# A seven-product expert layer: each product in its own PSUM bank, or summed there in chains

## The chip, the cores and the metric

The kernel runs on one core of a Trainium2 chip. The metric is device time in microseconds (us) for one execution; lower is better. Engines are named as in the profile: PE is TensorE, DVE is VectorE, ACT is ScalarE, POOL is GpSimd, SP is the queue that issues the DMAs. PSUM is the memory that TensorE writes; it has eight banks.

## The reference

Block-sparse attention gives `x` (3072 tokens, 512 features); a mixture of eight experts follows, in which every token goes through every expert and a balanced weight `P` sums the results.

```python
def _moe_ref(x, w_gate, w1, w2):
    ...
    for e in range(E):                       # 8 experts
        h = np.maximum(x @ w1[e], 0.0)       # 512 -> 1024
        ye = h @ w2[e]                       # 1024 -> 512
        out += P[:, e:e + 1] * ye
    return out.astype(np.float32)
```

Results are needed to float32 accuracy.

## The kernel before, in words

Attention comes first (lines 318 to 705) and writes `x` in pieces to DRAM. The rest, which this case is about, is the expert part: 32 blocks `i`, one for each of 8 experts and 4 batches of 768 tokens. Stage one of a block is `x @ w1` with its Relu, stage two is `h @ w2`.

Each matrix product is done by a scheme of Strassen's kind (Winograd's form): the operands are cut into two by two quadrants, and seven products of sums of quadrants replace eight. The products are numbered 0 to 6. Each float32 operand is held as a high and a low float16 half, so one product is three matmuls for each chunk of 128 (high-high, high-low, low-high).

**Stage one** (`stage1`, line 936) goes by four quarters `qi` of 128 hidden units. A product is 6 matmuls of 128x384 (line 945) into a bank of the pool `ps_h` (4 banks). The products come in the order of `PORDER`: 0, 1, 5, 6, 3, 4, 2. Each is combined with what came before: ACT copies product 0 out (line 990, tile a1), and DVE adds the others by `comb` (line 955), seven instructions a quarter since product 4 is read twice. Relu runs on ACT. From the four quadrants of the hidden layer (a1, u3, r11, c21) POOL makes the sums that stage two needs (`add`, lines 1017 and 843), and `emit` makes the halves of each operand of stage two: the high half on ACT (line 965), the low half on POOL for products 2, 3 and 5 and on DVE for the others (line 975; line 969 for product 1, whose Relu is folded in).

**Stage two** (`stage2`, line 1043) goes by product and by three chunks `ci` of 128 tokens. A chunk is 12 matmuls of 128x256 (line 1058) into a bank of `ps_y` (4 banks). DVE then adds it, times the token's weight, to the accumulators in SBUF (line 1079). The table `USES` says where to: product 0 goes to four quadrants in two instructions 512 wide, 5 to three, 4 to two, the others to one. For the first expert ACT copies product 0 out instead (line 1076).

**Order.** While stage two of block `i` runs, stage one of block `i + 1` is issued between its products (lines 1123 to 1174): products 0 and 1, quarter 0, product 5, quarter 1, products 6 and 3, quarter 2, products 4 and 2, quarter 3. Work that is less urgent (low halves, POOL sums, the weights of the next expert) is put in lists (`Slots`, line 758); `tick` is called after each product with an estimate of its cost and issues what fits, and `need` issues at once what the next step must have. Tile's scheduler then orders each engine's instructions by a simulated time line; on the chip each engine takes them in that order.

**At each change of expert** 2 MB of weights are loaded for each stage (`load_w`, line 152). DVE finds their largest value (line 170) and POOL reduces it over partitions (line 177); the scale follows from that. POOL makes sums of quadrants (line 836), and the seven operands are split into halves on ACT (line 821) and DVE (line 825): `split_w1` while the last block of the old expert runs, `split_w2` after it. The second weight is loaded into the buffer of the first, once all of that has been split.

Of the kernel before, what the change touches and what calls it, by code (L numbers as in the profile page):

```python
# [10 lines left out]
F32 = mybir.dt.float32  # L11
# [18 lines left out]
PORDER = (0, 1, 5, 6, 3, 4, 2)  # L30
NHT = 30
NU = 8
LOP = (2, 3)
LOPE = (2, 3, 5)
NLE = 99
# [24 lines left out]
def tile_sparse_attention_moe(  # L60
# [151 lines left out]
    def first_steps():  # L212
# [39 lines left out]
        for n, p in enumerate(PORDER[:4]):  # L252
            at(NTILE - NC * (4 - n // 2 * 2), lambda p=p: load_x1(0, p))
        split(TS1, 6, temp)
        split(TS1, 3, d)
        split(TS2, 4, c)
# [481 lines left out]
    ps_y = mpool("ps_y", 4, space=PSUM)  # L738
# [111 lines left out]
    def split_w1(e):  # L850
        a, s3 = wr["a"], wr["s3"]

        def one(p, src):
            queue_split(w1p[p], src, ("w1", e, p))

        one(0, a[0, 0])
        queue_sum(a[0, 0], a[1, 0], a[0, 0], ("w1", e, 5))
        one(1, a[0, 1])
        queue_sum(a[0, 1], a[0, 1], a[0, 0], ("w1", e, 2))
        one(5, a[0, 0])  # L860
        one(6, s3)
        one(3, a[1, 1])
        one(4, a[1, 0])
        one(2, a[0, 1])
# [70 lines left out]

    def stage1(i, qi):
        fs = slice(qi * P, (qi + 1) * P)
        lop = LOPE if i < NLE else LOP

        def product(p):  # L940
            slots.need(("w1", i // B, p))
            ps = ps_h.tile([P, 512], F32, tag="ph", name=f"p{p}_{i}_{qi}")[:, :TH]
            for kc in range(KH):
                for m, (l, r) in enumerate(((0, 0), (0, 1), (1, 0))):
                    nc.tensor.matmul(  # L945
                        ps, lhsT=w1p[p][:, l, kc, fs], rhs=xp[p][:, r, kc],
                        start=(kc == 0 and m == 0), stop=(kc == KH - 1 and m == 2),
                    )
            return ps
# [9 lines left out]
        def emit(p, src, relu=False, delay=0):  # L959
# [4 lines left out]
            def high():  # L964
                nc.scalar.activation(h[:, 0], src, AF.Relu if relu else AF.Copy)  # L965

            def low():
                if relu:
                    nc.vector.scalar_tensor_tensor(
                        out=h[:, 1], in0=src, scalar=0.0, in1=h[:, 0],  # L970
                        op0=ALU.max, op1=ALU.subtract,
                    )
                else:
                    eng = nc.gpsimd if p in lop else nc.vector
                    eng.tensor_tensor(out=h[:, 1], in0=src, in1=h[:, 0], op=ALU.subtract)  # L975
# [5 lines left out]
            if p in lop:  # L981
# [7 lines left out]
        a1 = fresh("a1")  # L989
        nc.scalar.activation(a1, product(0), AF.Copy, scale=HDOWN)  # L990
        tick(0, 1)
        r11 = fresh("r11")
        comb(r11, product(1), a1)
        nc.scalar.activation(r11, r11, AF.Relu)
        emit(0, r11)
        tick(1, 2)
        comb(a1, product(5), a1)
        tick(1, 0)
        u3 = fresh("u3")
        comb(u3, product(6), a1)  # L1000
        tick(1, 0)
        slots.settle(i, qi - 1)
        c21 = fresh("c21")
        comb(c21, product(3), u3)
        emit(1, c21, relu=True)
        tick(1, 1)
        p5 = product(4)
        comb(u3, p5, u3)
        comb(a1, p5, a1)
        nc.scalar.activation(u3, u3, AF.Relu)  # L1010
        emit(3, u3)
        tick(2, 2)
        comb(a1, product(2), a1)
        nc.scalar.activation(a1, a1, AF.Relu)  # L1014

        def add():
            nc.gpsimd.tensor_tensor(out=s1, in0=a1, in1=u3, op=ALU.add)  # L1017
            sub(a1, a1, r11)
            slots.need((("h", i, 0), i, qi))
            sub(r11, s1, r11)  # L1020
            slots.need((("h", i, 1), i, qi))
            nc.scalar.activation(c21, c21, AF.Relu)
            sub(c21, c21, r11)

        s1 = fresh("s1")
        slots.add(add, (("sum", i), i, qi), 1, act=0.41, pool=3.9)
        emit(4, s1, delay=SD[0])
        emit(6, a1, delay=SD[1])
        emit(5, r11, delay=SD[2])
        emit(2, c21, delay=SD[3])  # L1030
        tick(1, 1)

    USES = {
        0: ((0, None), (1, None)),
        1: ((0, 0),),
        5: ((0, 1), (1, None)),
        6: ((1, None),),
        3: ((1, 0),),
        4: ((0, 1), (1, 1)),
        2: ((0, 1),),  # L1040
    }

    def stage2(i, p):
        e, b = divmod(i, B)
        if p not in (0, 1, 3):
            slots.need(("sum", i))
        slots.need(("h", i, p))
        slots.need(("w2", e, p))
        if b == 0 and e:
            slots.need(("pwe", e))  # L1050
        for ci in range(CH):
            t0 = b * NC + ci
            ts = (t0, t0 + CH)
            py = ps_y.tile([P, 512], F32, tag="py", name=f"py_{i}_{p}_{ci}")[:, :DH]
            tsl = slice(ci * P, (ci + 1) * P)
            for kc in range(KF // 2):
                for m, (l, r) in enumerate(((0, 0), (0, 1), (1, 0))):
                    nc.tensor.matmul(  # L1058
                        py, lhsT=hs[i, p, kc][:, l, tsl], rhs=w2p[p][:, r, kc],
                        start=(kc == 0 and m == 0), stop=(kc == KF // 2 - 1 and m == 2),  # L1060
                    )
            if p == 0 and e == 1:
                for t in ts:
                    nc.scalar.activation(
# [140 lines left out]
```

## Time and profile before

| what | value |
|---|---|
| runs shown | 2587.79, 2589.89, 2609.31 us; median 2589.89 us |
| profiled execution, its span | 2589.7 us |
| chain that ended last, by engine | PE 59%, DVE 15%, POOL 9%, issue 8%, DMA 6%, ACT 2% |
| mean granted TensorE clock | 0.944 |
| HBM | 140.54 MB read, 17.30 MB written, 61 GB/s over the span |

In a line of the groups stand line, engine, operation, what is written and read (names of the program, buffer numbers left out), the shapes and the count; then the busy time in us, the mean duration of one in ns, and the idle time of the engine just before, with what ended it. In a line of the waits stand who waited for whom, the us in total, how many times, and the longest. In a line of the order of time stand the start and duration in us, the engine, the line and the instruction, and in brackets the idle time before it and what ended that. "Issue" is time in which the engine waited for nothing that the profile shows.

### The profile page before, as it was taken

How to read it: one execution, taken by the hardware profiler on the slowest of the kernel's cores; microseconds unless marked ns; L12 is line 12 of the kernel's file. 1: busy time of each engine (PE TensorE's matmuls, PEld its weight loads, DVE VectorE, ACT ScalarE, POOL GpSimd, SP SyncE). 2: the span in 40 equal slices, each digit the busy share in tenths (PEclk: the TensorE clock that was granted, in tenths of full speed). 3: DMA queues.
4: the chain of work that ended last, by engine and by line, in shares of the span. 5: the costliest groups of instructions: out<-in, count | busy, mean ns of one | idle time of the engine just before them, and what ended most of it. 6: DMA issues, size and time to landing. Idle time of an engine off the chain costs nothing.

```text
span 2589.7 us, 46975 instructions
## 1 busy us (share of the span) xinstructions
PE 2361.4 (91%) x18270; PEld 1678.2 (65%) x18270; DVE 2009.5 (78%) x3747; ACT 1277.7 (49%) x2234; POOL 1559.8 (60%) x1387
## 2 busy tenths in 40 slices
PE   6999999897879979998998999899989998998999
PEld 3656666564656657765775677577657765776777
DVE  6768788675767788788778878877887788778876
ACT  4466767664445544444454444444444444444442
POOL 4557687763754476457556655755476557556653
PEclk9967879787989989999999999999999999999999
DMA  5679999996111221122121212211221122121211
GB/s 167 141 154 190 190 186 197 182 203 134 58 68 44 76 76 44 44 76 76 48 82 62 87 47 76 76 44 44 76 76 44 44 76 76 57 73 60 84 68 50
DMA packets 363924, 236.38 MB, mean 91 GB/s; under 512 B 303772, under 2 KB 316084, under 8 KB 363700
## 3 DMA queue, kind: packets, MB, share of 16 engines
q1 hardware_dynamic: 362128, 230.59, 34.9%
q10 hardware_dynamic: 1572, 2.78, 0.6%
q8 instruction: 143, 2.34, 0.4%
q14 instruction: 81, 0.66, 0.1%
HBM read 140.54 MB, written 17.30 MB: 61 GB/s over the span
## 4 chain that ended last, share of the span: by engine, by line
PE 59%; DVE 15%; POOL 9%; issue 8%; DMA 6%; ACT 2%; SPq 0%; DVEq 0%; POOLq 0%; ACTq 0%
PE py L1058 24%; PE p L945 22%; PE sc L513 4%; PE sc L510 4%; PE u L577 3%; DMA pt<-ph 3%; POOL r L836 3%; DMA r<-in_moe_w_dram 3%; DVE mx_w L170 2%; DVE h L975 2%; DVE acc L1079 2%; POOL h L975 2%; DVE w1p L825 1%; DVE u L955 1%; DVE a L955 1%
## 5 line engine op out<-in xcount | busy, mean ns | idle before, releaser
L1058 PE MATMUL py<-w2p,h 128*128 128x256 f16 x8064 | 974.6, 276 | 59.9 <-DVE acc L1079 21.3
L1058 PEld LDWEIGHTS <-h 128*128 128x128 f16 x8064 | 795.0, 99 | 221.6 <-issue 23.9
L1079 DVE SCALAR_TENSOR_TENSOR acc<-py,spare,acc 128x256 f32<-128x256 f32 (+1 forms) x840 | 457.8, 580 | 50.6 <-PE py L1058 49.4
L945 PE MATMUL p<-arena 128*128 128x384 f16 x2304 | 424.5, 334 | 70.9 <-DVE c L955 34.2
L975 POOL TENSOR_TENSOR h<-u,h 128x384 f16<-128x384 f32 x128 | 135.0, 1055 | 571.4 <-ACT h L965 474.2
L945 PEld LDWEIGHTS <-w1p 128*128 128x128 f16 x3072 | 302.5, 99 | 215.6 <-issue 41.5
L945 PE MATMUL p<-x,w1p 128*128 128x384 f16 x2304 | 407.4, 328 | 15.7 <-ACT a L990 13.3
L945 PEld LDWEIGHTS <-arena 128*128 128x128 f16 x2304 | 229.3, 100 | 213.1 <-issue 89.4
L965 ACT ACTIVATE h<-c 128x384 f16<-128x384 f32 x256 | 132.2, 522 | 351.8 <-DVE c L955 275.3
L536 POOL TENSOR_TENSOR ph<-pe,ph 128x768 f16<-128x768 f32 x144 | 259.8, 1818 | 69.1 <-ACT ph L532 51.9
L518 DVE CUSTOM_DVE_ANT_0 pe<-sc,mask 128x768 f32<-128x768 f32 x192 | 182.6, 954 | 112.3 <-PE sc L513 92.1
L955 DVE SCALAR_TENSOR_TENSOR a<-p,a 128x384 f32<-128x384 f32 x384 | 210.7, 549 | 20.2 <-PE p L945 15.0
L523 ACT ACTIVATE pe<-pe,nm 128x768 f32<-128x768 f32 x192 | 174.9, 928 | 98.6 <-DVE nm L522 86.2
L510 PE MATMUL sc<-k,q 128*128 128x512 f32 (+1 forms) x384 | 199.2, 519 | 18.8 <-DVE nm L518 17.2
L513 PE MATMUL sc<-k,q 64*128 64x512 f32 (+1 forms) x384 | 200.8, 524 | 0.0
L965 ACT ACTIVATE h<-r 128x384 f16<-128x384 f32 x256 | 132.2, 521 | 97.9 <-POOL r L843 94.3
L1017 POOL TENSOR_TENSOR s<-a,u 128x384 f32<-128x384 f32 x128 | 141.0, 1101 | 51.0 <-ACT a L1014 51.0
L577 PE MATMUL u<-vh,pt 128*128 128x66 f16 x2304 | 149.3, 211 | 17.8 <-DMA pt<-ph 16.9
L843 POOL TENSOR_TENSOR r<-s,r 128x384 f32<-128x384 f32 x128 | 149.0, 1164 | 23.6 <-issue 14.0
L945 PE MATMUL p<-arena,w1p 128*128 128x384 f16 x768 | 149.5, 330 | 14.9 <-DVE a L955 9.6
L577 PEld LDWEIGHTS <-pt 128*128 128x128 f16 x3456 | 140.1, 109 | 30.4 <-DMA pt<-ph 18.7
L843 POOL TENSOR_TENSOR c<-c,r 128x384 f32<-128x384 f32 x128 | 149.5, 1168 | 9.2
(155 smaller groups left out, 3439.7 us busy)
## 6 DMA issues: line engine op xcount, KB each, us to landing
arena<-xd SPq DMA_DIRECT2D x124, 384.0 KB, 3.8
x<-xd SPq DMA_DIRECT2D x93, 384.0 KB, 4.1
r<-in_moe_w_dram SPq DMA_DIRECT2D x16, 2048.0 KB, 8.8
arena<-in_q_dram SPq DMA_DIRECT2D x16, 384.0 KB, 3.5
arena<-in_k_dram SPq DMA_DIRECT2D x16, 384.0 KB, 4.1
arena<-in_v_dram SPq DMA_DIRECT2D x4, 1536.0 KB, 8.6
xd<-xs_t SPq DMA_DIRECT2D x16, 384.0 KB, 3.0
out_dram<-acc SPq DMA_DIRECT2D x24, 256.0 KB, 2.0
```

The source lines that it names most:

```text
L510: nc.tensor.matmul(sc[:, lo:hi], lhsT=q1[:, qc], rhs=k1[:, lo:hi], start=True, stop=False)
L513: nc.tensor.matmul(sc[:, lo:hi], lhsT=q2[:D, qc], rhs=k1[:D, lo:hi], start=False, stop=True)
L518: nc.vector.tensor_tensor_reduce(out=pe, in0=sc[:, :S], in1=masks[c], scale=1.0, scalar=-FMAX, op0=ALU.add, op1=ALU.max, accum_out=nm,)
L536: eng.tensor_tensor(out=lo, in0=pe, in1=hi, op=ALU.subtract)
L577: nc.tensor.matmul(uv[:, c], lhsT=a[:, ci * NC + kc, :], rhs=w[:, h, kc, :], start=(kc == 0 and m == 0), stop=(kc == NC - 1 and m == 2),)
L843: nc.gpsimd.tensor_tensor(out=out, in0=x, in1=y, op=ALU.subtract)
L945: nc.tensor.matmul(ps, lhsT=w1p[p][:, l, kc, fs], rhs=xp[p][:, r, kc], start=(kc == 0 and m == 0), stop=(kc == KH - 1 and m == 2),)
L955: nc.vector.scalar_tensor_tensor(out=t, in0=ps, scalar=HDOWN, in1=other, op0=ALU.mult, op1=ALU.add)
L965: nc.scalar.activation(h[:, 0], src, AF.Relu if relu else AF.Copy)
L975: eng.tensor_tensor(out=h[:, 1], in0=src, in1=h[:, 0], op=ALU.subtract)
L1058: nc.tensor.matmul(py, lhsT=hs[i, p, kc][:, l, tsl], rhs=w2p[p][:, r, kc], start=(kc == 0 and m == 0), stop=(kc == KF // 2 - 1 and m == 2),)
L1079: nc.vector.scalar_tensor_tensor(out=dst, in0=src, scalar=c, in1=dst, op0=ALU.mult, op1=ALU.add)
```

## The change

Stage one keeps three banks a quarter: x, y and z. Product 0 opens x; products 5, 6 and 3 are added onto it in PSUM (no `start` flag), and ACT reads the running sum after each (r11's share, a1, u3, c21). Product 1 alone is in y and is added to r11 by DVE. Product 4 opens z and product 2 is added onto it; DVE adds z to u3 after the first and to a1 after the second. So three `comb` instructions are left of seven, and four ACT reads stand in place of one. The order is 0, 1, 5, 4, 6 (the first half of a quarter), then 3, 2 (the second half).

Stage two does the same with the chains 0, 5, 6, 3 and 4, 2: each running sum is read once, 256 wide, into one quadrant. `ps_x` has three banks, one for each chunk, and `ps_y` one, for product 1 and for a few small products elsewhere.

The two halves of a quarter are issued apart, with a product of stage two between. The low half of product 3 moves from POOL to DVE; the activations and first weights of products 4 and 6 change places in their order.

```diff
-PORDER = (0, 1, 5, 6, 3, 4, 2)
+PORDER = (0, 1, 5, 4, 6, 3, 2)
-LOPE = (2, 3, 5)
+LOP = (2, 5)
...
     ps_h = mpool("ps_h", 4, space=PSUM)
-    ps_y = mpool("ps_y", 4, space=PSUM)
+    ps_x = mpool("ps_x", 3, space=PSUM)
+    ps_y = mpool("ps_y", 1, space=PSUM)
...
+        def copied(nm, ps, func=AF.Copy):
+            t = fresh(nm)
+            nc.scalar.activation(t, ps, func, scale=HDOWN)
+            return t
...
+        def first():
+            x = bank_of("x")
+            product(0, x, True)
+            r11 = copied("r11", x)
+            tick(0, 1)
+            y = bank_of("y")
+            product(1, y, True)
+            comb(r11, y, r11)
+            relu(r11)
+            emit(0, r11)
+            tick(1, 2)
+            product(5, x)
+            a1 = copied("a1", x)
+            tick(0, 1)
+            z = bank_of("z")
+            product(4, z, True)
+            tick(0, 0)
+            product(6, x)
+            u3 = copied("u3", x)
+            comb(u3, z, u3)
+            relu(u3)
+            slots.settle(i, qi - 1)
+            emit(3, u3)
+            tick(1, 3)
+            pend[i, qi] = x, z, r11, a1, u3
+
+        def second():
+            x, z, r11, a1, u3 = pend.pop((i, qi))
+            product(3, x)
+            c21 = copied("c21", x, AF.Relu)
+            emit(1, c21)
+            tick(0, 2)
+            product(2, z)
+            comb(a1, z, a1)
+            relu(a1)
...
+    AFTER = {0: (0, 0), 1: (0, 0), 5: (0, 1), 6: (1, 1), 3: (1, 0), 4: (1, 1), 2: (0, 1)}
+    OPENS = {0: "x", 1: "y", 4: "x"}
+    FROM = {5: 0, 6: 5, 3: 6, 2: 4}
+    chain = {}
...
+        if p in OPENS:
+            pool = ps_y if OPENS[p] == "y" else ps_x
+            py = pool.tile([P, 512], F32, tag="py", name=f"py_{i}_{p}_{ci}")[:, :DH]
+        else:
+            py = chain.pop((i, FROM[p], ci))
...
+        if e == 0 and p in (0, 5, 6, 3):
+            nc.scalar.activation(dst, py, AF.Copy)
+        else:
+            c = 1.0 if e == 0 else pwe[e][:, t : t + 1]
+            nc.vector.scalar_tensor_tensor(
+                out=dst, in0=py, scalar=c, in1=dst, op0=ALU.mult, op1=ALU.add
+            )
...
-        stage2(i, 0)
-        stage2(i, 1)
-        quarter(0)
+        stage2(i, 0, 0)
+        stage2(i, 0, 1)
+        stage2(i, 1, 0)
+        stage2(i, 0, 2)
+        stage2(i, 1, 1)
+        first(0)
...
-        stage2(i, 5)
+        stage2(i, 1, 2)
+        products(i, 5)
         if last:
             parts[0]()
-        quarter(1)
-        stage2(i, 6)
-        stage2(i, 3)
+        second(0)
+        first(1)
+        products(i, 6)
+        second(1)
+        products(i, 3)
         if last:
             parts[1]()
-        quarter(2)
-        stage2(i, 4)
-        stage2(i, 2)
+        first(2)
+        products(i, 4)
+        second(2)
+        first(3)
+        products(i, 2)
         if last:
             parts[2]()
-        quarter(3)
+        second(3)
```

For the first block, whose stage one has no stage two beside it, both halves of a quarter are issued one after the other.

201 lines of the change are left out of this document (81 added, 120 removed).

## The prediction

> **What bounds the kernel now.** I read the page's head first, then the busy time by stages, then who TensorE waited for, over the expert part and inside one of its stalls, and last the instructions in order of time.
>
> ```profile
> span 2589.7 us, 46975 instructions
> PE 2361.4 (91%) x18270; PEld 1678.2 (65%) x18270; DVE 2009.5 (78%) x3747; ACT 1277.7 (49%) x2234; POOL 1559.8 (60%) x1387
> ```
>
> TensorE is busy for 91% of the span, and attention, which the change leaves alone, fills the first 600 us or so. The stages of the rest (columns: stretch, length, then busy time and instructions of PE, PEld, DVE, ACT, POOL, then granted clock, DMA):
>
> ```profile
> 600.00:800.00 200.00, 155.41 (x1167) 107.84 (x1168) 139.60 (x275) 81.31 (x156) 108.38 (x98) 0.87 0.24 70
> 870.00:990.00 120.00, 99.41 (x697) 69.49 (x696) 93.48 (x164) 54.22 (x103) 73.44 (x71) 0.94 0.17 59
> 1115.00:1215.00 100.00, 82.94 (x603) 59.16 (x601) 86.00 (x151) 40.35 (x74) 60.92 (x58) 0.97 0.22 75
> 1215.00:1357.00 142.00, 142.00 (x1085) 105.95 (x1084) 110.01 (x192) 69.20 (x132) 85.23 (x81) 1.00 0.17 57
> 1357.00:1457.00 100.00, 83.42 (x603) 59.44 (x601) 86.00 (x151) 40.37 (x74) 60.96 (x59) 0.97 0.21 74
> 1599.00:1699.00 100.00, 82.59 (x597) 58.66 (x595) 85.89 (x151) 40.35 (x74) 59.94 (x58) 0.97 0.22 74
> 1842.00:1942.00 100.00, 82.53 (x594) 58.57 (x593) 85.85 (x151) 39.81 (x74) 60.11 (x58) 0.97 0.21 73
> 2084.00:2184.00 100.00, 82.43 (x596) 58.65 (x594) 85.89 (x151) 40.33 (x74) 60.19 (x57) 0.97 0.21 74
> 2326.00:2426.00 100.00, 87.38 (x647) 63.39 (x646) 88.55 (x149) 46.65 (x87) 66.63 (x64) 0.98 0.17 54
> ```
>
> Between expert changes (1215 to 1357) TensorE never idles, at full clock: 1085 matmuls in 142 us, 7.64 per us, so nothing can be won there. Around each expert change, where the next expert's weights are scaled, summed and split, some 100 us hold only 597 matmuls, work for 597 / 7.64 = 78.1 us: 21.9 us are lost, 17.4 idle and 4.5 at a lower clock. The six 100 us rows lose 21.1, 21.1, 21.9, 22.3, 22.0 and 15.3 us, the first change (870 to 990) 28.8 us. In units of the 21.9 us change that is 5 + 0.7 + 1.3 = 7.0 changes. The start (600 to 800) idles another 44.6 us at clock 0.87. Only these stalls can pay for the change. Who they wait for, over the whole expert part and then inside 1599 to 1699:
>
> ```profile
> PE p L945 <- DVE c L955: 34.2, 14, 5.1
> PE p L945 <- DVE a L955: 25.9, 16, 6.8
> PE py L1058 <- DVE acc L1079: 21.3, 17, 2.0
> ```
>
> ```profile
> PE p L945 <- DVE c L955: 5.3, 2, 5.1
> PE py L1058 <- DVE acc L1079: 2.9, 2, 1.5
> PE p L945 <- DVE u L955: 2.5, 2, 2.3
> PE p L945 <- DVE a L955: 2.3, 2, 1.7
> PE py L1058 <- ACT h L965: 1.6, 2, 1.5
> PE p L945 <- ACT a L990: 1.4, 1, 1.4
> PE py L1058 <- DVE h L975: 1.4, 1, 1.4
> ```
>
> Of the 17.4 us, VectorE is named for 14.4. But it is late for two reasons, which order of time tells apart:
>
> ```profile
> 1650.55 1.15 ACT L821 ACTIVATE w2p<-t,sw 128x1024 f16<-128x1024 f32 x1 [4.40 <-POOL t L836]
> 1656.37 2.08 PE L945 MATMUL p<-arena 128*128 128x384 f16 x6 [5.12 <-DVE c L955]
> ```
>
> ```profile
> 1677.56 4.83 DVE L170 TENSOR_REDUCE mx_w<-r 128x1 f32<-128x512 f32 x8
> 1692.46 0.15 DVE L180 TENSOR_SCALAR ma_w<-ma_w 128x1 f32<-128x1 f32 x1 [3.62 <-POOL ma_w L177]
> 1693.13 1.61 PE L945 MATMUL p<-arena 128*128 128x384 f16 x6 [2.30 <-DVE u L955]
> ```
>
> The 5.1 us stall stands at the end of a chain POOL, ACT, DVE: GpSimd's weight sums are late, ScalarE waits 4.40 us for one, VectorE's split waits behind that, and the combination that TensorE wants is queued behind the split. The 2.3 us stall is VectorE waiting 3.62 us for GpSimd's reduction over partitions. The 1.5 us of L1079 comes behind eight reductions in a row (4.83 us). The rest of VectorE's share (2.3 for a, the other 1.4 of acc, 1.4 for h) is plain backlog.
>
> **The change part by part.** The durations:
>
> ```profile
> L1079 DVE SCALAR_TENSOR_TENSOR acc<-py,spare,acc 128x512 f32<-128x512 f32 x336 | 238.1, 739 | 7.7 <-PE py L1058 7.7
> L1079 DVE SCALAR_TENSOR_TENSOR acc<-py,spare,acc 128x256 f32<-128x256 f32 x504 | 228.1, 474 | 43.0 <-PE py L1058 41.8
> L955 DVE SCALAR_TENSOR_TENSOR u<-p,u 128x384 f32<-128x384 f32 x128 | 70.8, 553 | 27.7 <-PE p L945 24.5 <-PE py L1058 0.5
> L975 POOL TENSOR_TENSOR h<-u,h 128x384 f16<-128x384 f32 x128 | 135.0, 1055 | 571.4 <-ACT h L965 474.2 <-ACT a L990 41.9 <-ACT w2p L821 40.8
> L975 DVE TENSOR_TENSOR h<-s,h 128x384 f16<-128x384 f32 x128 | 112.1, 876 | 46.9 <-ACT h L965 46.6
> L975 DVE TENSOR_TENSOR h<-r,h 128x384 f16<-128x384 f32 x128 | 91.2, 713 | 17.5 <-ACT h L965 16.9
> L969 DVE SCALAR_TENSOR_TENSOR h<-c,h 128x384 f16<-128x384 f32 x128 | 74.5, 582 | 14.5 <-ACT h L965 14.5
> L990 ACT ACTIVATE a<-p 128x384 f32<-128x384 f32 x128 | 61.6, 481 | 75.5 <-PE p L945 61.7 <-POOL h L975 12.6
> ```
>
> *Stage two, reads.* For the seven later experts 336 wide and 504 narrow reads (466.2 us) become 588 narrow ones: 588 x 228.1 / 504 = 266 us. Gain for VectorE 200 us.
> *Stage one, combinations.* Seven a quarter become three (r11, u3, a1): 512 of 896 go, at 0.55 us, 282 us.
> *Low halves.* That of product 3 moves from GpSimd (135 us off it) to VectorE, between 0.713 and 0.876 us each, 91 to 112 us; I take 100, in the middle. That of product 1 becomes a plain subtraction at the same bounds instead of 582 ns: 17 to 38 us, I take 25.
> VectorE in all: -200 - 282 + 125 = -357 us. The expert part is 13,440 matmuls / 7.64 = 1759 us of TensorE work, so 0.203 us leave VectorE for each us of it: 78.1 x 0.203 = 15.9 us in the stretch from 1599, from 85.9 to 70.
> *ScalarE.* Three more copies out of PSUM a quarter and one Relu fewer, 2 x 128 x 0.481 = 123 us more; no row shows a Relu out of PSUM, and the copy at 481 ns is the nearest for both bounds. ScalarE is busy 40 of 100 us in the stretch, so its work is hidden; its lateness is not, see the next edit.
> *The new wait.* Product 5 adds into the bank that holds product 0, so it must wait for ScalarE's copy of it; 6 waits so for 5, 3 for 6, and 2 for VectorE's read of 4. Queued behind a waiting matmul is everything else on TensorE. Undisturbed it costs nothing:
>
> ```profile
> 1735.69 3.09 PE L945 MATMUL p<-arena 128*128 128x384 f16 x18
> 1736.87 0.49 ACT L990 ACTIVATE a<-p 128x384 f32<-128x384 f32 x1 [1.66 <-PE p L945]
> 1738.62 1.14 PE L945 MATMUL p<-arena,w1p 128*128 128x384 f16 x6
> ```
>
> Matmuls start (3.09 - 1.14) / 12 = 0.1625 us apart and six take 1.14, so product 0 (the first six of the 18) ends at 1736.83, the copy runs from 1736.87 to 1737.36, and the thirteenth matmul, where product 5 would stand with product 1 between, starts at 1737.64: 0.28 us to spare. Links 6 to 3 and 4 to 2 have a whole stage-two product (36 matmuls) between. Without cover a link costs 0.16 (1.14 less six starts) + 0.04 + 0.49 + some 0.05 for the signal back, an estimate = 0.74 us. Lower bound 0 (a wait can't gain), upper bound in the third rival. Between expert changes I take 0; in a change, where ScalarE stood 4.40 us for GpSimd, I take 1.5 us, a third of that.
> The Trainium skill, "PSUM — Partial Sum Buffer", in its summary of rules for kernel authors, says to read PSUM in another bank than the one the matmuls write, which speaks against a chain that is read after each product. With every link bare it would cost 4 x 128 x 0.74 = 379 us; by the rows above it is covered.
> *Banks of stage two.* Four rotating become three chains and one bank for product 1. Successive products of a chain stand at least two products apart, the reads take 0.47 us; the one bank of product 1 has a third of product 0 (12 matmuls, 1.31 us) or the first half of a quarter between its uses. Nothing, except in the last block, about 0.5 us once; with the first expert's four extra ScalarE reads I put 2 us for all of it.
> *Moved steps.* The load of the next second weight is issued after five products of a quarter instead of seven, on the same SP queue; it still waits for the last split of the first weight, so I give it nothing. The activations of products 4 and 6 change place in their loading order: same bytes. The second half of a quarter comes later by one product of stage two (3.9 us); its first consumer, product 1 of the next block, has product 2 and two thirds of product 0 in between.
>
> **The sum.** Of one change's stalls the backlog goes (2.3 + 1.4 + 1.4 = 5.1 us) and half of the 5.1 us one (2.5), since GpSimd loses 78.1 x 135 / 1759 = 6.0 us of work and VectorE 15.9 before it; the reduction's 2.3, the eight reductions' 1.5 and ScalarE's 3.0 stay. With fewer gaps 2 of the 4.5 us at a lower clock go. Less the new 1.5: 8.1 us, times 7.0 = 57. At the start, where POOL and loads bind too, 10 of 44.6 us. 57 + 10 - 2 = 65, and 2589.7 - 65 = 2525 us. The profiled execution's own time is its span of 2589.7 us; the median of the runs shown is 2589.9, so no shift.
> The Trainium skill, "TensorE: Matmul & The Clock Gate", section "HAM oscillation — how this bites in real kernels", puts the harm at idle gaps over about 3.4 us. The trace disagrees: six matmuls took 2.08 us after a 5.12 us gap, and 1.61 us after one of only 2.30 us. By the rule only the first slows the clock and 3 rather than 2 us would go per change, 2518 us; I go by the rows.
>
> **The rivals.**
> *All of VectorE's stalls go* (0.20). For it: VectorE falls to 70 of 100 us, and with its weight work planned into free time the sums on GpSimd start earlier. Against: two stalls are waits for GpSimd. 14.4 + 4.5 = 18.9 a change, times 7.0 = 132, and 12 at the start: 2446 us.
> *The stalls were never VectorE's own* (0.20). Only its backlog in front of a and acc goes, 3.7 us, less the new 1.5: 2.2 x 7 = 15: 2575 us. For it: the chain through POOL and the reduction. The change then doesn't do what it is for.
> *ScalarE is late in the links* (0.15; the other side). It is in order, and often stands before a result of GpSimd:
>
> ```profile
> ACT h L965 <- POOL s L1017: 170.4, 116, 4.0
> ACT h L965 <- POOL r L843: 94.3, 112, 14.7
> ```
>
> A copy queued behind such a wait (170.4 / 116 = 1.47 us) comes 1.47 - 0.28 = 1.19 us late for TensorE. If one in three of the 256 short links (0 to 5, 5 to 6) is caught, 101 us: 2525 + 101 = 2626 us. It decides against the change from 65 / 256 = 0.25 us a short link. Against it: in the undisturbed quarter the copy starts 0.04 us after its product.
> *Every link bare* (0.03): 379 - 65 = 314 more, 2904 us; it needs an order of instructions that puts nothing between, and the program puts something in each.
>
> **How the numbers follow.** The forecast of 2525 us has 0.42, its own range 2495 to 2560. About 1% is what a measurement of this kernel can tell from no change (2564 to 2616 us). Faster: 0.42 + 0.20 + 0.03 of the second rival = 0.65. Same: the other 0.17 and 0.02 of the third = 0.19. Slower: 0.13 + 0.03 = 0.16. The range from 2435 to 2610 holds the first two rivals and leaves out most of the third and the fourth.
>
> **What would show it.** Right: VectorE near 1650 us in all and GpSimd near 1425; the stretches between changes still at 7.64 matmuls per us; changes with about 13 us lost instead of 22, the waits for VectorE's combinations mostly gone and that for the partition reduction still there. Wrong: waits of stage-one matmuls on ScalarE's copies spread through the stretches between changes (third rival), or unchanged losses at the changes (second).

## The result and the profile after

| kernel | median, us | runs | ratio to before, 95% interval |
|---|---|---|---|
| before | 2591.22 | 4 (2587.79 to 2609.31) | |
| after | 2637.03 | 4 (2633.79 to 2640.76) | 1.0159, 1.0126 to 1.0191 |

The change makes the kernel slower, by 1.59% or 41 us (46 us between the medians), where 65 us less were forecast; the range (2435 to 2610) does not hold it. The profiled execution after has a span of 2639.0 us, at a mean granted clock of 0.935 (0.944 before).

The engines' sums, from the head of the page after:

```profile
PE 2379.9 (90%) x18270; PEld 1688.8 (64%) x18270; DVE 1697.1 (64%) x3051; ACT 1384.1 (52%) x2514; POOL 1448.3 (55%) x1259
```

VectorE lost 312 us, GpSimd 112, ScalarE gained 106: the change did what it says. The time is not in these sums. Two stages of the kernel after (busy windows, columns as in the prediction), one between expert changes and one at a change:

```profile
1745.00:1860.00 115.00, 115.00 (x882) 86.05 (x881) 67.89 (x112) 58.80 (x119) 56.05 (x53) 1.00 0.17 50
1866.00:1976.00 110.00, 88.46 (x615) 61.30 (x613) 72.95 (x122) 51.66 (x96) 61.66 (x59) 0.94 0.25 82
```

Between changes TensorE is as full as before: 882 matmuls in 115 us, 7.67 per us. At a change 615 matmuls are work for 615 / 7.67 = 80.2 us, so 29.8 us are lost where the kernel before lost 21.9. Counted so, the seven changes after lose 31.3, 29.0, 30.2, 29.9, 29.8, 30.6 and 15.6 us, against 28.8, 21.1, 21.1, 21.9, 22.3, 22.0 and 15.3 before: 44 us more, of the 49 us between the two profiled executions. The last change, at which only a second weight is left to load and so only one reduction runs, loses no more than before. Whom TensorE waited for in the expert part after (waits: us in total, times, longest):

```profile
PE x L947 <- DVE a L957: 32.0, 12, 5.8
PE py L1074 <- DVE acc L1091: 28.2, 15, 3.7
PE x L947 <- ACT u L963: 27.5, 12, 12.9
PE z L947 <- ACT c L963: 23.6, 21, 3.2
...
PE z L947 <- DVE ma_w L180: 16.0, 6, 2.9
```

No single engine is named for most of it. (The largest wait for a copy, 12.9 us, stands once at the start.) GpSimd's own waits lead further; first those of before, then those of after:

```profile
POOL ma_w L177 <- issue: 53.2, 9, 6.0
...
POOL ma_w L177 <- DVE ma_w L176: 48.1, 6, 8.6
```

```profile
POOL ma_w L175 <- issue: 89.4, 15, 6.3
POOL s L1030 <- issue: 42.8, 6, 7.3
```

All 15 reductions of weights over partitions in the expert part (two for each change, one more at the start) are preceded after by 5.8 to 6.3 us in which GpSimd does nothing and waits for nothing the profile shows, and each is followed by another 6.8 to 7.6 us, some of them put down to other engines. The trace holds an instruction MODIFY_POOL_CONFIG at the start of both gaps. In the kernel before, six of the gaps ahead of the reduction are put down to VectorE's late maximum (48.1 us). One such standstill in order of time, the first of a change, before:

```profile
1610.62 1.00 POOL L1017 TENSOR_TENSOR s<-a,u 128x384 f32<-128x384 f32 x1 [4.75 <-ACT a L1014]
...
1615.68 0.92 POOL L975 TENSOR_TENSOR h<-c,h 128x384 f16<-128x384 f32 x1
1625.19 0.38 POOL L177 PARTITION_ALL_REDUCE ma_w<-ma_w  x1 [8.60 <-DVE ma_w L176]
1632.50 1.24 POOL L975 TENSOR_TENSOR h<-u,h 128x384 f16<-128x384 f32 x1 [6.92 <-ACT w2p L821]
1633.70 1.97 POOL L1017 TENSOR_TENSOR s<-a,u 128x384 f32<-128x384 f32 x1
...
1635.71 0.52 ACT L965 ACTIVATE h<-s 128x384 f16<-128x384 f32 x1 [3.38 <-POOL s L1017]
```

and after:

```profile
1896.19 1.00 POOL L1030 TENSOR_TENSOR s<-a,u 128x384 f32<-128x384 f32 x1 [4.61 <-ACT a L967]
...
1901.45 0.92 POOL L979 TENSOR_TENSOR h<-c,h 128x384 f16<-128x384 f32 x1
1908.31 0.38 POOL L175 PARTITION_ALL_REDUCE ma_w<-ma_w  x1 [5.94 <-issue]
1915.47 3.09 POOL L835 TENSOR_TENSOR r<-r 128x256 f32<-128x256 f32 x4 [6.79 <-DVE h L979]
...
1922.62 0.99 POOL L1030 TENSOR_TENSOR s<-a,u 128x384 f32<-128x384 f32 x1
1923.64 0.52 ACT L975 ACTIVATE h<-s 128x384 f16<-128x384 f32 x1 [6.02 <-POOL s L1030]
1927.98 1.43 PE L947 MATMUL x<-x,w1p 128*128 128x384 f16 x6 [1.96 <-ACT u L963]
```

GpSimd stands for 15.9 us before (1615.68 + 0.92 to 1632.50) and 13.1 us after, and the sum s that ScalarE needs follows the previous sum by 23.1 us before and by 26.4 us after (seven us of weight sums now stand between). ScalarE, in order, stands at the high half of s for 3.38 us before and 6.02 us after; its longest wait there in the whole expert part was 4.0 us (the row in the prediction) and is now:

```profile
ACT h L975 <- POOL s L1030: 155.5, 114, 7.0
```

Behind it stand three weight splits and the copy u that the next product of the chain waits for.

Most of the extra loss stands at the second reduction of a change, that of the next first weight:

| stretch | matmuls | lost, us (length less the matmuls at 7.64 or 7.67 per us) | granted clock |
|---|---|---|---|
| before, 1599 to 1684 | 510 | 18.2 | 0.98 |
| before, 1684 to 1710, second reduction at 1692.05 | 165 | 4.4 | 0.93 |
| after, 1866 to 1950 | 530 | 14.9 | 0.98 |
| after, 1950 to 1976, second reduction at 1958.50 | 85 | 14.9 | 0.80 |

There VectorE stands for the reduction's result, and TensorE behind VectorE, as in the prediction's row at 1693.13, but for 5.31 us instead of 2.30:

```profile
1958.91 0.15 DVE L178 TENSOR_SCALAR ma_w<-ma_w 128x1 f32<-128x1 f32 x1 [5.40 <-POOL ma_w L175]
...
1959.59 2.08 PE L947 MATMUL x<-arena 128*128 128x384 f16 x6 [5.31 <-DVE a L957]
```

A second stall of 3.52 us follows, behind the gap after the reduction (7.28 us, then s, its halves, and a read of stage two). Over the expert part VectorE waits 69.9 us for the reductions' results, 35.3 before.

The Trainium skill, "GPSIMD Engine Reference", section "2.1 Instruction dispatch", says that the first call of a freshly loaded GpSimd kernel pays some 6 us (5.95) that no instruction of the profile shows. The trace agrees, with 5.94 us at the reduction above and 5.8 to 6.3 at all 15, and adds that it is paid at every reduction, and that the way back to the next ordinary instruction costs another 6.8 to 7.6 us. The prediction had no term for it.

So theory A: the chains lose by GpSimd's standstill, which they cover worse. Theory B: the chains leave too few banks and have too many links (a link is a product that must wait for the read of the one before it in its chain), and would lose without it.

### The profile page after: what moved, and what is told of

Read it like the earlier page. It is cut to its first block, busy times and chain, and to the rows that moved or that the text cites. A ratio compares the mean times of both kernels' runs of the same rounds, so it can differ in the third digit from the quotient of the medians.

```text
span 2639.0 us, 45728 instructions
## 1 busy us (share of the span) xinstructions
PE 2379.9 (90%) x18270; PEld 1688.8 (64%) x18270; DVE 1697.1 (64%) x3051; ACT 1384.1 (52%) x2514; POOL 1448.3 (55%) x1259
## 4 chain that ended last, share of the span: by engine, by line
PE 46%; DVE 10%; POOL 6%; issue 5%; DMA 5%; ACT 2%; SPq 0%; POOLq 0%; ACTq 0%
PE py L1074 24%; PE x L947 13%; PE z L947 7%; DMA r<-in_moe_w_dram 4%; DVE h L979 3%; PE y L947 3%; POOL r L835 3%; DVE mx_w L168 2%; DVE acc L1091 1%; DVE w1p L824 1%; DVE w2p L824 1%; POOL s L1030 1%; DVE a L957 1%; POOL t L835 1%; POOL a L842 1%
## 5 line engine op out<-in xcount | busy, mean ns | idle before, releaser
L1074 PE MATMUL py<-w2p,h 128*128 128x256 f16 x8064 | 1005.9, 276 | 59.0 <-DVE acc L1091 28.2
L1030 POOL TENSOR_TENSOR s<-a,u 128x384 f32<-128x384 f32 x128 | 131.4, 1027 | 744.6 <-ACT a L967 687.5
L1091 DVE SCALAR_TENSOR_TENSOR acc<-py,spare,acc 128x256 f32<-128x256 f32 x588 | 271.2, 477 | 142.9 <-PE py L1074 141.6
L947 PE MATMUL x<-x,w1p 128*128 128x384 f16 x1536 | 303.4, 335 | 39.8 <-ACT u L963 27.5
L947 PE MATMUL x<-arena 128*128 128x384 f16 x1536 | 298.9, 332 | 38.0 <-DVE a L957 32.0
L979 DVE TENSOR_TENSOR h<-s,h 128x384 f16<-128x384 f32 x128 | 117.1, 915 | 115.3 <-ACT h L975 114.7
L947 PE MATMUL z<-x,w1p 128*128 128x384 f16 x768 | 149.4, 332 | 32.9 <-DVE u L957 16.9
L947 PE MATMUL z<-arena,w1p 128*128 128x384 f16 x768 | 145.9, 326 | 24.3 <-ACT c L963 23.6
L842 POOL TENSOR_TENSOR c<-c,r 128x384 f32<-128x384 f32 x128 | 160.4, 1253 | 10.0
L963 ACT ACTIVATE u<-x 128x384 f32<-128x384 f32 x128 | 62.4, 487 | 186.0 <-PE x L947 185.8
```

The costliest lines, as they stand in the source:

```text
L842: nc.gpsimd.tensor_tensor(out=out, in0=x, in1=y, op=ALU.subtract)
L947: nc.tensor.matmul(ps, lhsT=w1p[p][:, l, kc, fs], rhs=xp[p][:, r, kc], start=(opens and kc == 0 and m == 0), stop=(kc == KH - 1 and m == 2 ...
L1074: nc.tensor.matmul(py, lhsT=hs[i, p, kc][:, l, tsl], rhs=w2p[p][:, r, kc], start=(p in OPENS and kc == 0 and m == 0), stop=(kc == KF // 2 ...
L1091: nc.vector.scalar_tensor_tensor(out=dst, in0=py, scalar=c, in1=dst, op0=ALU.mult, op1=ALU.add)
```

## The experiments

Times are medians; a ratio is to the kernel before on the same chip, with its 95% interval; one hundredth of it, a point, is 26 us. The kernel before was at 2591.1 to 2601.5 us there.

### No reduction on GpSimd: e1 (after), e2 (before)

```diff
-            gpsimd.partition_all_reduce(a, a, P, ReduceOp.max)
+            nc.tensor.matmul(pc[:, :1], lhsT=ones, rhs=a, start=True, stop=True)
...
-            vector.tensor_scalar(a, a, TINY, HUGE, ALU.max, ALU.min)
+            vector.tensor_scalar(a, pc[:, :1], 1.0 / P, TINY, ALU.mult, ALU.max)
```

> The changed kernel, with one edit: the scale of each expert weight (but for the first one) comes from the mean of the partitions' largest values, by a matmul with ones into a ps_h bank, in place of GpSimd's maximum over partitions. Theory A (GpSimd's change of configuration around its reduction, some 6 us before and 7 us after, is what the changed kernel runs into: VectorE waited 69.9 us for it against 35.3): about 13 of the 29 us lost at each expert change go, and some 10 us at the start, 2637 - 7 x 13 - 10 = 2536 us, below the kernel before. Theory B (the chains leave too few banks, so that TensorE stalls on any late read): the gain is only the reduction's own 2.3 us stall and its slow clock, as in the kernel before, 2637 - 7 x 4 = 2609 us.

> The kernel before with the same edit as the run on the changed kernel: the weights' scales by a matmul with ones (mean of the partitions' largest values) in place of GpSimd's reduction. Theory A: here the change of configuration was mostly hidden under VectorE's backlog, so only the one 2.3 us stall with its slow clock goes, 5 us at each of 7 changes, and a few us at the start: 2591 - 40 = 2550 us, some 15 us over the changed kernel with this edit. Theory B: 2555 us, and the changed kernel with this edit stays 50 us behind it.

Measured: e1 2517.15 us, 0.9684 (0.9637 to 0.9731); e2 2520.47 us, 0.9712 (0.9666 to 0.9759). The same stretch at a change, e1 and then e2:

```profile
1540.00:1640.00 100.00, 88.19 (x657) 63.62 (x656) 78.49 (x124) 55.98 (x105) 67.89 (x61) 1.00 0.28 90
```

```profile
1540.00:1640.00 100.00, 89.57 (x653) 64.51 (x652) 90.14 (x151) 43.32 (x81) 67.93 (x64) 0.97 0.24 79
```

They lose 14.3 (100 - 657 / 7.67) and 14.5 us (100 - 653 / 7.64). So the 15 reductions cost 2.88 points (75 us, 5.0 each) before and 4.75 points (123 us, 8.2 each) after. The difference of 1.87 points (0.7 either way) is all of the measured 1.59 and a little more. Theory A is right on the loss, but its times were too high, that of e2 by 30 us: in the kernel before the standstill was not covered either. And without the reductions the chains gain nothing that can be measured, where theory A wanted 15 us and the prediction more.

### Each pair of chains alone: e3, e4, and without reductions e7, e8

e3 is the change without stage two's part, in the new order; e4 the change without stage one's part, in the old order.

Against the kernel after, e3:

```diff
-    ps_x = mpool("ps_x", 3, space=PSUM)
-    ps_y = mpool("ps_y", 1, space=PSUM)
+    ps_y = mpool("ps_y", 4, space=PSUM)
...
-        j, k = AFTER[p]
-        t = ts[j]
+        for j, k in USES[p]:
+            t = ts[j]
```

and e4, with `stage1` as before:

```diff
-PORDER = (0, 1, 5, 4, 6, 3, 2)
+PORDER = (0, 1, 5, 6, 3, 4, 2)
...
-        first(0)
+        quarter(0)
```

e7 and e8 are these two with the edit of e1.

> Stage one as in the changed kernel (chains x, z, the two halves of a quarter apart, low half of product 3 on VectorE), stage two with a bank for each chunk and the reads of the kernel before (four rotating banks, 512 wide reads). Theory A: VectorE keeps 200 us more work than in the changed kernel, so part of its backlog still covers GpSimd's change of configuration: between the two, about 2610 us. Theory B with the links of stage one at fault: as slow as the changed kernel or slower, 2635 to 2660 us.

> Stage one as in the kernel before; stage two with the chains and the single bank for product 1 of the changed kernel (products 0 and 1 alternate by chunk, all before quarter 0). Theory A: VectorE loses 200 us of work, GpSimd none; some of the cover of the change of configuration goes: about 2600 us. Theory B with stage one at fault: the backlog gain without the links, about 2565 us; with stage two's banks at fault: 2630 us.

> The stage-one chains alone (2732 us, 46 us lost at each change), with the weight scales from TensorE. Theory A (what is lost beyond the kernel before is only GpSimd's configuration change): 2505 to 2540 us, as the kernels before and after with this edit. Theory L (the links need an early VectorE and ScalarE; with the wide reads of stage two still on VectorE they come late at each change whatever GpSimd does): 2580 to 2640 us.

> The stage-two chains alone (2650 us), with the weight scales from TensorE. Theory A: 2505 to 2535 us. Theory B (three chains and one bank leave stage two too few banks, so that TensorE waits for the reads of L1076 whatever GpSimd does): 2550 to 2600 us.

Measured: e3 2732.1 us, 1.0531 (1.0479 to 1.0583); e4 2650.55 us, 1.0216 (1.0178 to 1.0253); e7 2610.0 us, 1.004 (0.9997 to 1.0083); e8 2495.29 us, 0.9618 (0.9555 to 0.968). Every guess for e3 and e4 was too low. In e8 theory B falls: stage two's chains have banks enough, and gain about a point (24 us, the intervals overlap a little) over e2, more than theory A allowed. In e7 theory L holds: stage one's chains cost even with no standstill. TensorE's waits in e7 are many and mostly short, for VectorE's reads of stage two and for ScalarE's copies u and a and its high halves:

```profile
PE py L1084 <- DVE acc L1106: 37.7, 36, 3.3
PE x L957 <- ACT u L973: 36.7, 42, 3.3
PE py L1084 <- ACT h L985: 27.0, 16, 6.7
PE x L957 <- ACT a L973: 13.5, 9, 3.2
```

### Whose wait it is: e5

e1 with GpSimd's reduction beside TensorE's, on a copy that nobody reads.

```diff
+                vector.tensor_scalar(idle, a, 1.0, None, ALU.mult)
+                gpsimd.partition_all_reduce(idle, idle, P, ReduceOp.max)
```

> The kernel after with the weight scales from TensorE (2517 us), and beside it GpSimd's reduction again, on a copy that nobody reads: VectorE no longer waits for its result, GpSimd still pays the 6 us before and 7 us after it. The 15 reductions cost 120 us in the kernel after. Theory V (the price is VectorE standing at the head of its queue for the result): almost all of the gain stays, 2517 to 2535 us. Theory G (the price is GpSimd standing still for 13 us, its sums late, and ScalarE and VectorE behind them): most of the 120 us comes back, 2595 to 2640 us. Half and half: 2560 to 2590 us.

Measured: 2645.85 us, 1.021 (1.0135 to 1.0284), all of it back. Theory G holds: the price does not hang on VectorE's wait for the reduction's result (the 2.3 us that the prediction saw, 5.31 us after). Without that wait GpSimd's standstill costs as much by another way. TensorE now waits for ScalarE's copy in the chain, from the second change on 8.5 to 9.3 us at each second reduction and 1.5 to 2.1 us at each first:

```profile
PE x L961 <- ACT a L977: 76.3, 15, 9.3
```

### VectorE's low halves: e6

```diff
-LOP = (2, 5)
+LOP = (2, 5, 6)
```

> The kernel after with the weight scales from TensorE (2517 us), and the low half of product 6 moved from VectorE (152 us in all, 1.19 us each where 0.54 is the shortest) to GpSimd. Theory C (the chains gain nothing because VectorE's low halves with two SBUF operands run at half speed beside GpSimd, and TensorE waits 57 us for low halves and for sums queued behind them): half of these waits goes, 2480 to 2500 us. Theory D (GpSimd is then late itself, 1459 + 140 us): 2520 to 2550 us.

Measured: 2508.22 us, 0.9675 (0.9606 to 0.9744), beside e1's 0.9684: no difference, and neither range holds it. VectorE lost 134 us, GpSimd gained 97, and the time stayed. TensorE's waits for VectorE's low halves and reads fell from 56.7 to 19.1 us, as theory C wanted, but its waits for ScalarE's four copies rose from 36.2 to 56.4 us. So less work on VectorE alone does not pay here; the edit does not part VectorE's load from GpSimd's.

### The same standstill where nothing else is late: e9 to e12

e1 and e2 with 14 idle reductions between the changes. `Behind` is issued behind GpSimd's last subtraction of a quarter (h<-c), but in the trace it starts one instruction earlier at all 14 places, between the last two subtractions; `ahead` stands directly ahead of s.

```diff
     eng.tensor_tensor(out=h[:, 1], in0=src, in1=h[:, 0], op=ALU.subtract)
+    if p == 2 and (i, qi) in SPOTS:          # behind
+        gpsimd.partition_all_reduce(idle, src[:, :1], P, ReduceOp.max)
...
+    if (i, qi) in SPOTS:                     # ahead
+        gpsimd.partition_all_reduce(idle, a1[:, :1], P, ReduceOp.max)
     nc.gpsimd.tensor_tensor(out=s1, in0=a1, in1=u3, op=ALU.add)
```

> The kernel after with the weight scales from TensorE (2517 us), and 14 idle reductions on GpSimd between the expert changes, where nothing else is late: each stands in a quarter behind GpSimd's last subtraction (c), its result is read by nobody. The next sum s then starts 4.4 + 1.2 + 13.5 + 1.2 = 20.3 us after the one before instead of 14, 6.3 us late. Theory P (the price of a standstill is set by how late it makes the next s, after which ScalarE's queue stands; 5 to 6 us are free): 0 to 2 us each, 2517 to 2545 us. Theory K (the chains hand any standstill on to TensorE): 6 us each, 2600 us.

> The same 14 idle reductions in the kernel after with the weight scales from TensorE, directly ahead of a sum s and only once its operand is there, so that s is 13.5 us late. Theory P: 7 to 9 us each, 2615 to 2645 us. Theory K: 13 us each, 2700 us. If place does not matter: as with the reductions behind c.

> The kernel before with the weight scales from TensorE (2520 us), the 14 idle reductions behind c: the next s comes 21.5 instead of 14 us after the one before, 7 us late. Theory P: 0 to 2 us each, 2520 to 2550 us. Theory K (the kernel before takes a standstill better): 2520 us, no price.

> The kernel before with the weight scales from TensorE, the 14 idle reductions directly ahead of s, 13.5 us late. Theory P: 7 to 9 us each, as in the kernel after, 2620 to 2645 us. Theory K: clearly less than in the kernel after, 3 to 5 us each, 2560 to 2590 us.

| run | us | ratio | each standstill, over e1 or e2 | TensorE's loss in the 30 us around one, mean |
|---|---|---|---|---|
| e9 after, behind | 2618.19 | 1.0103 (1.008 to 1.0126) | 4.19 points / 14 = 7.8 us | 7.0 us |
| e10 after, ahead | 2629.66 | 1.012 (1.0069 to 1.017) | 8.1 us | 7.1 us |
| e11 before, behind | 2591.58 | 0.9991 (0.9966 to 1.0016) | 5.2 us | 4.2 us |
| e12 before, ahead | 2699.09 | 1.0412 (1.0382 to 1.0441) | 13.0 us | 11.9 us |

(The fourth column is known to about 1 us either way. The last is read from the traces: 30 us less the matmuls in them at 7.67 per us, 7.64 for the kernel before.) Theory P falls: behind is not nearly free, and ahead is dearer before than it allows. Theory K holds only behind; ahead it is the other way round. The kernel after pays 8 us at both places. The kernel before pays 5 or 13, and its real reductions stand next to where it pays 5 (between h<-c and h<-u, 1615 to 1632 above). That agrees with the 5.0 and 8.2 us of the real ones. Why it is dearer after, at one of the 14 places, in order of time, in e9:

```profile
1222.76 0.38 POOL L944 PARTITION_ALL_REDUCE idle<-c  x1 [6.01 <-PE x L964]
...
1226.32 2.11 PE L964 MATMUL x<-arena 128*128 128x384 f16 x12
1228.27 1.14 PE L964 MATMUL y<-arena 128*128 128x384 f16 x6
1229.24 1.47 PE L1093 MATMUL py<-w2p,h 128*128 128x256 f16 x12
1231.95 0.90 POOL L996 TENSOR_TENSOR h<-c,h 128x384 f16<-128x384 f32 x1 [8.82 <-issue]
...
1233.84 0.52 ACT L992 ACTIVATE h<-s 128x384 f16<-128x384 f32 x1 [8.58 <-POOL s L1049]
...
1235.65 0.47 ACT L980 ACTIVATE a<-x 128x384 f32<-128x384 f32 x1
...
1236.17 2.08 PE L964 MATMUL x<-x,w1p 128*128 128x384 f16 x6 [5.46 <-ACT a L980]
```

and in e11:

```profile
1947.39 7.48 PE L1077 MATMUL py<-w2p,h 128*128 128x256 f16 x67
...
1954.71 3.09 PE L962 MATMUL p<-arena 128*128 128x384 f16 x18
1957.63 1.14 PE L962 MATMUL p<-arena,w1p 128*128 128x384 f16 x6
1959.78 0.52 ACT L982 ACTIVATE h<-s 128x384 f16<-128x384 f32 x1 [10.65 <-POOL s L1036]
...
1962.61 1.25 PE L1077 MATMUL py<-w2p,h 128*128 128x256 f16 x5 [3.84 <-DVE acc L1098]
```

In e11 ScalarE stood longer here (10.65 us) than in e9 (8.58), yet TensorE's stall is shorter. From when ScalarE ran dry TensorE worked on for 9.64 us in e11 (1959.78 - 10.65 = 1949.13, to 1962.61 - 3.84 = 1958.77): stage two's products, then four of stage one into the four banks of `ps_h`. In e9 it had work for 5.45 us (1233.84 - 8.58 = 1225.26, to 1236.17 - 5.46 = 1230.71), until it came to product 6, whose bank waited for the copy of product 5 (`a`), and that copy stood behind the high half of s. At this place what the chain gives up is run-ahead: work that TensorE can still do while its readers stand.

That is only part of the difference. With the clock that falls after either stall, TensorE loses about as much around these two places (7.2 us in e9, 7.1 in e11). What e11 saves it saves at every second place, where it loses 1.2 to 4.1 us and waits 1.6 us for a copy; at those places of e9 TensorE waits 4.3 to 5.9 us for a high half that ScalarE makes for stage two, and no link is in play. Of e9's 14 stalls six are at a link, seven at a high half, one at a read of stage two.

### Is it the order? e13, e14, e16

e13 is the kernel before with its quarters cut into halves and issued as in the change (the seven products keep their old order, 6 before 4, and products 0 and 1 of stage two do not alternate); e14 is that without the reductions; e16 (second diff) is the kernel after with its order cut otherwise.

```diff
-        quarter(1)
+        half(0)
+        half(1)
         stage2(i, 6)
+        half(1)
         stage2(i, 3)
```

```diff
-        products(i, 5)
+        stage2(i, 5, 0)
+        second(0)
+        stage2(i, 5, 1)
+        stage2(i, 5, 2)
         if last:
             parts[0]()
-        second(0)
+        stage2(i, 6, 0)
         first(1)
...
```

> The kernel before with the change's order alone: a stage-two product between the two halves of a quarter, banks, reads and low halves as before, and GpSimd's reductions in the same place of its queue as before. Theory O (the order makes the standstill dearer): most of the 47 us appears, 2620 to 2645 us. Theory L (the links make it dearer): as before, 2580 to 2600 us.

> The same with the weight scales from TensorE. Both theories: with no standstill the order costs little, 2515 to 2540 us beside 2520 us with the old order. Then e13 less this is the price of the standstill in the new order: Theory O 100 to 120 us, Theory L 70 us.

> The kernel after with its stage-two products cut otherwise: between any two halves stand two or three of their thirds (1.3 us each), where before two pairs of halves stood next to each other. GpSimd's reductions stand where they stood, and the chains are the same. Theory O: the price of the standstill falls from 8 us to 5 or 6 us, 2590 to 2615 us. Theory L: as after, 2630 to 2645 us.

Measured: e13 2562.11 us, 0.9847 (0.9784 to 0.991); e14 2510.0 us, 0.965 (0.9612 to 0.9689); e16 2644.26 us, 1.0179 (1.0128 to 1.0231). Theory O falls twice: the order alone is a gain of 1.5 points, where a loss was expected, and another cut changes nothing. (Its standstills cost 2.0 points for 2.9, a difference within the intervals.) All corners together, as ratios:

| kernel | with GpSimd's reductions | without | the 15 standstills, points |
|---|---|---|---|
| before | 1 | 0.9712 | 2.9 |
| new order alone | 0.9847 | 0.965 | 2.0 |
| new order and stage one's chains | 1.0531 | 1.004 | 4.9 |
| the whole change | 1.0159 | 0.9684 | 4.8 |
| stage two's chains alone | 1.0216 | 0.9618 | 6.0 |

Stage one's chains (with the low half and the order of products that go with them) are what costs, 3.9 points by themselves and 2.9 more by the standstills. On top of them stage two's chains give 3.6 points back (e7 to e1); by which wait was not tested. Alone these are dear with reductions: in e4's trace the reduction of the second weight falls between h<-u and s at every change, the dear place of e12.

### Is it that ScalarE makes the copies? e17, e18

```diff
-            nc.scalar.activation(t, ps, func, scale=HDOWN)
+            nc.vector.tensor_scalar(t, ps, HDOWN, None, ALU.mult)
```

> The kernel after with the weight scales from TensorE (2517 us), and the four copies out of the chains' banks in a quarter made by VectorE instead of ScalarE: 512 x about 0.5 us, 250 us more on VectorE (1712 to 1960), as much less on ScalarE. It is the base for the next run. TensorE waited 36 us for ScalarE's copies, 13 of it once at the start, and 57 us for VectorE: 2510 to 2545 us; no theory hangs on it.

> The same with the 14 idle reductions behind c (with ScalarE's copies 7.2 us each, in the kernel before 5.1 us). Theory S (a standstill is dearer in the kernel after because ScalarE, in order, stands at the high half of s and the chains' copies stand behind it): with the copies on VectorE 4 to 5.5 us each, 55 to 75 us over the run before. Theory Q (the chains as such, or the low half that VectorE took over): 7 us each or more, 95 to 120 us.

Measured: e17 2566.73 us, 0.9886 (0.9828 to 0.9944); e18 2675.0 us, 1.0299 (1.0229 to 1.0369): 4.1 points, 7.6 us each. e17, meant as a base, is itself 2 points over e1, above its guess. Theory S's range for e18 is missed, theory Q's holds it. The rows say why:

```profile
1253.63 0.52 ACT L995 ACTIVATE h<-s 128x384 f16<-128x384 f32 x1 [8.85 <-POOL s L1052]
...
1254.18 0.90 DVE L999 TENSOR_TENSOR h<-s,h 128x384 f16<-128x384 f32 x1 [7.76 <-ACT h L995]
...
1255.07 0.54 DVE L983 TENSOR_SCALAR a<-x 128x384 f32<-128x384 f32 x1
...
1255.66 0.80 PE L964 MATMUL x<-x,w1p 128*128 128x384 f16 x2 [6.06 <-DVE sw L192]
```

VectorE stands behind s as well, one step further, at its low half, and the copy behind that. (The wait is put down to sw; the copy `a` ends last, at 1255.61.) Both engines that read PSUM in this kernel stand in line behind GpSimd, so the copy is late whichever of the two makes it: e18 did not free the copy, and so does not clear the links. At every second place TensorE waits for a high half of ScalarE's, here too (3.1 to 4.1 us).

### The best version: e15

e8 with the reduction ahead of the router's exponentials on TensorE too.

```diff
-            nc.gpsimd.partition_all_reduce(m, m, P, ReduceOp.max)
-            nc.vector.tensor_scalar(m, m, -1.0, None, ALU.mult)
+            nc.tensor.matmul(pm[:, :1], lhsT=ones, rhs=m, start=True, stop=True)
+            nc.vector.tensor_scalar(m, pm[:, :1], -1.0 / P, None, ALU.mult)
```

> The stage-two chains alone with the weight scales from TensorE (2495 us), and the reduction ahead of the router's exponentials on TensorE too (its shift is the mean of the partitions' largest values, not the largest of all). In the kernel after with the weight scales from TensorE a wait of 12.9 us stood there; some 8 to 12 us go: 2480 to 2490 us, the best version. If that wait is covered here: 2495 us.

Measured: 2480.81 us, 0.9544 (0.9493 to 0.9595), 121 us under the kernel before on its chip and the fastest of all; the intervals of e8 and e15 overlap, so the last edit's own gain is not certain.

## Why the prediction was wrong, point by point

*Where time can be won.* Right: TensorE stays full between changes (7.67 per us), and nearly all of the difference, 44 of 49 us, arises at the changes.

*The sums of the engines.* Near: VectorE 1697 for 1650, GpSimd 1448 for 1425, ScalarE +106 for +123. The durations of VectorE's instructions added up fell by 364 us (2187 to 1823), as forecast (357); the page counts time in which two of them overlap once, and 52 us less of them overlap after. Within that sum the low halves came out 159 us longer in all, for 125. It is not the moved one, which took 0.631 us where I took 0.78, but two that VectorE had already, those of product 6 (0.953 before) and product 0 (0.713):

```profile
L979 DVE TENSOR_TENSOR h<-a,h 128x384 f16<-128x384 f32 x128 | 150.7, 1177 | 7.3 <-ACT h L975 7.1
L979 DVE TENSOR_TENSOR h<-r,h 128x384 f16<-128x384 f32 x128 | 130.9, 1023 | 19.5 <-ACT h L975 17.4
L979 DVE TENSOR_TENSOR h<-u,h 128x384 f16<-128x384 f32 x128 | 80.7, 631 | 77.6 <-ACT h L975 77.2
```

*"The reduction's 2.3 ... stay."* This is the step that failed. I priced the reductions at one wait of VectorE's, 2.3 us, and left it unchanged. Their price was 75 us in the kernel before, 5.0 us each, and became 123 us, 8.2 each. The one wait did not stay either: at the same reduction it grew from 2.30 to 5.31 us, and the loss around it from 4.4 to 14.9. Two things hid the price: "issue" is named on GpSimd only, which is off the path by its busy share, and six of the fifteen waits were put down to VectorE's late maximum. Two rows that the prediction quotes are its traces: the 3.62 us wait for L177, and ScalarE's 170.4 us for s.

*The backlog goes (5.1 and 2.5 a change), with 2 us of clock.* Mostly wrong. Ahead of the second reduction a change loses 3.3 us less than before (14.9 for 18.2). But without standstills both kernels lose 14.3 to 14.5 us in the stretch shown, and e6 takes 134 us more off VectorE for nothing. Stage two's reads alone gain about a point (e8), which is 3.4 us a change; stage one's edits take it back.

*The new wait, 0 between changes and 1.5 us at each.* Right between changes. At changes mis-sized: between 1866 and 1976 TensorE waited 5.3 us for ScalarE's copies (3.3 for c, 2.0 for u) instead of 1.5, and in e9 5.46 us behind one standstill. The 0.28 us to spare was reckoned from an undisturbed quarter; what counted at that place is for how long TensorE can go on when the readers stand, 9.64 us in e11 and 5.45 in e9. A price of 15 standstills was needed, not a share of 256 links.

*Moved steps.* Mis-sized at nothing: the order alone gains 1.5 points (e13), for which I had no term.

*The rivals.* The third, late links, comes nearest with 2626 us, and its place (a chain product behind ScalarE's wait for s) is what e9 shows at six of 14 places and e5 at the second reductions. But its mechanism is not quite it: it put the lateness in every third link, by the mean wait of 1.47 us, where a few long ones do it (3.7 to 5.5 us in e9), and in the kernel after itself the longest stall of a change stands behind VectorE. That its number is near the measured one is luck.

*What stays open.* Stage one's edits were not taken apart further: how much of their 3.9 points without any standstill is links, and how much the low half of product 3 on VectorE. That a standstill is dearer after is measured; why it is stays partly open. That run-ahead is the cause is argued from one pair of places in e9 and e11 and explains at most the stalls at links; no run gave the chains another bank, since all eight are in use. Why stage two's high halves come too late in the new order of work was not tested.

## What to carry to other kernels

Before costing an edit by the load of engines, find out for how long the engine that sets the end can run on when its consumers stand: in the rows above rotating banks bought that time, and a chain that is read after each product spent it. Look for engines that stand still under "issue", even off the path, and price their standstill by taking the instruction away; here that one edit won 2.9 points in the kernel before (e2), where the change lost 1.6. And a standstill's price depends on what stands next in the queue: in the kernel before the same idle reduction cost 5 us among a quarter's last subtractions and 13 us directly ahead of a sum that another engine waits for.

## What the runs showed of the hardware

- GpSimd stands some 13 us for each reduction over partitions between other work: 5.8 to 6.3 us ahead of it, 0.4 us for the reduction itself, 6.8 to 7.6 us behind it in the kernel after, 13.4 us in the mean, and as much when nobody reads the result (e5, 13.4). Here the scale can as well follow from the mean of the partitions' maxima: a matmul with ones took the reduction's place and gained 2.9 and 4.8 points (e2, e1).
- VectorE's subtraction of two SBUF operands, 128x384, takes 0.55 us while GpSimd stands and up to 1.35 us while GpSimd subtracts (e9):

```profile
1019.97 0.55 DVE L996 TENSOR_TENSOR h<-u,h 128x384 f16<-128x384 f32 x1
...
1034.57 1.19 POOL L853 TENSOR_TENSOR c<-c,r 128x384 f32<-128x384 f32 x1
1034.83 1.35 DVE L996 TENSOR_TENSOR h<-a,h 128x384 f16<-128x384 f32 x1
```

The Trainium skill, "SBUF — State Buffer", section "Who interferes with whom", says that a VectorE instruction with two SBUF inputs contends with a GpSimd instruction that reads SBUF. The trace agrees, 0.55 against 1.35 us. The low half in the last row is that of product 6, whose mean grew from 0.953 to 1.177 us with the change. That more of them now fall beside GpSimd's work is likely, and no run shows it alone.
